# A new first-batch start, spread-out boundary scores and all squares on VectorE in a gated-attention and feed-forward kernel

## The chip, the cores and the metric

The kernel runs on one core of a Trainium2 chip. The metric is the device time of one execution in microseconds (us). Times are medians over several executions of the same build. One execution of each kernel is recorded by the hardware profiler; its span is the length of that one execution.

Names used below: PE is TensorE, DVE VectorE, ACT ScalarE, POOL GpSimd, SP the sync engine, which does nothing here but issue DMA transfers. A `q` after an engine's name (SPq, ACTq) means an instruction of its sequencer, such as the issue of a DMA.

## The reference, cut to what matters

```python
# u, v: (8, 3008, 256); z: (8, 3008, 64); w_in: (256, 2048); w_out: (2048, 256); all float32
scores = (1.0 / S) * np.matmul(z, z.transpose(0, 2, 1))
attn = np.maximum(scores, 0.0) ** 2
x = (u * np.matmul(attn, v)).reshape(B * S, D)
h = x @ w_in
g = h * (1.0 / (1.0 + np.exp(-1.702 * h)))
return (g @ w_out)
```

The scores are symmetric. The kernel computes one triangle of tiles and gets the other by DMA transposes of the squared tiles.

## The kernel before

For each of the 8 batches there are six "chunks" of 512 rows. `attend(b, i)` multiplies squared scores with V for chunk i; the scores of chunk i+1 are computed between its matmuls. Then the feed-forward of the batch runs: `up_group` (x @ w_in, sigmoid on ACT, product on DVE) and `down` (g @ w_out). The scores of the next batch's first chunk stand among the last `down` steps. PSUM is split into three double tiles (`ps2`, shared by scores and `up_group`) and two single tiles (`ps1`, for attention and `down`).

```python
def load_z(b):                                  # cast-load by POOL, then one DMA transpose
    for c in range(2):
        pool.dma_start(zst[:, :NJ - 1, c, :], zd)
        ...
    sp.dma_start_transpose(ZT[b], zst...)

def load_v(b):                                  # loads by SP, six pieces through two buffers, cast on POOL
    ...
    sp.dma_start(vst[:, :full, :], ...)
    pool.tensor_copy(V16[b]..., vst...)

def load_u(b, i):                               # four loads by SP, then a transpose on DVE
    ...
    dve.transpose(ut..., uq...)

def scores(b, group, dve_relu=False):
    for i, jp in group:                         # PE: two 64-row matmuls per unit
        sc = ps2.tile([P, 2, CH], F32, ...)
        ...
    for ...:
        act.activation(rl, sc, AF.Relu, scale=csc)      # or DVE for every third, if dve_relu
        sq[0] += 1
        (pool if sq[0] % 4 == 0 else dve).tensor_tensor(a, rl, rl, ALU.mult)
        if cj > i:                              # the mirrored tile
            sp.dma_start_transpose(t..., a...)

# program
load_z(0); load_u(0, 0); load_v(0)
for g in split(pieces(0), FIRST):               # FIRST = [3, 3, 3, 3]
    scores(0, g, True)
for k in range(P // QW):                        # weights, cast-loads by POOL
    pool.dma_start(W1[k * QW:(k + 1) * QW], w1v[k])
pool.dma_start(W2, ...)
for b in range(B):
    for i in range(NCH):                        # attention, chunk by chunk
        if i + 1 < NCH: load_u(b, i + 1)
        ...
    if b + 1 < B:
        load_z(b + 1); load_v(b + 1); load_u(b + 1, 0)
    for q in range(HEAD, nup):
        up_group(b, q)
        if q >= LAGY: down(b, *downs.pop(0))
    nxt = split(pieces(0), FIRST) if b + 1 < B else []
    n = 0
    while downs or nxt:                         # the boundary: three units, three downs, ...
        if nxt and n % 3 == 0: scores(b + 1, nxt.pop(0), True)
        if downs: down(b, *downs.pop(0))
        n += 1
```

## Time and profile before

The time before was 1306.86 us (1302.85 to 1308.07, 4 runs).

These lines are from the profile page of the kernel before: busy time by engine, the busy tenths of PE and its clock in 40 slices of the span, the chain of work that ended last, and the two groups of squares. In a group line the figures after the bar are busy time and the mean ns of one instruction, then the idle time just before them.

```profile
span 1306.3 us, 19043 instructions
PE 1249.3 (96%) x7520; PEld 680.3 (52%) x7520; DVE 844.5 (65%) x820; ACT 728.8 (56%) x786; POOL 266.9 (20%) x237
PE   2799999999999999999989999999999999999998
PEclk9799999999999999999999999999999999999999
...
PE 92%; DVE 2%; DMA 1%; POOL 1%; issue 1%; ACT 1%; ACTq 1%; SPq 0%; POOLq 0%
...
L140 POOL TENSOR_TENSOR a<-rl 128x1024 f16<-128x1024 f16 x84 | 166.2, 1979 | 717.1 <-ACT rl L136 700.2
L140 DVE TENSOR_TENSOR a<-rl 128x1024 f16<-128x1024 f16 x252 | 230.9, 939 | 98.1 <-ACT rl L136 95.1
```

PE is the bound: 96% busy and 92% of the chain. The row of digits shows PE short of work in the first two slices (65 us); shorter losses do not show there. The waits of PE, in total, say what for:

```profile
engine line waited for: us in total, times, longest us
PE sc L126 <- DMA ZT<-zst: 19.6, 1, 19.6
PE sc L126 <- ACT rl L136: 19.5, 18, 4.3
PE o L174 <- POOL V_96 L97: 5.3, 3, 2.6
PE sc L126 <- DVE gt L231: 4.8, 7, 1.0
```

To say where PE time is lost I price every useful matmul at its undisturbed distance to the next (216 ns for 512 columns and 109 ns for 256 in the trace; for N columns I take N/2.4 + 2.5 ns, which fits both), count the paired 64-row score matmuls once per pair, and count dummies and PE transposes as nothing. That gives 1202.5 us in both kernels. "Lost" below is always a stretch of the trace minus this price of the matmuls that start in it. An attention phase without any visible gap still loses 2.76 us in this account.

| lost by PE, us | before |
|---|---|
| 0 to 60 us | 45.5 |
| 60 to 120 us (rest of the first batch's attention) | 2.0 |
| 120 to 1190 us (seven boundaries and steady work) | 50.8 |
| rest | 5.5 |
| total | 103.8 |

### The profile page before, as it was taken

What the parts mean: (1) busy time and instruction counts of PE and PEld (TensorE: products, weight loads), DVE (VectorE), ACT (ScalarE), POOL (GpSimd) and SP (SyncE); (2) the same over time, 40 slices, a digit from 0 to 9 for tenths busy, and PEclk for the clock granted to TensorE, in tenths of its full rate; (3) what the DMA queues carried; (4) which work ended last, traced back from release to release, by engine and by line L of the source; (5) the groups of instructions that cost most, each with busy time, mean ns of one, the idle gap of its engine ahead of it and who ended that gap; (6) DMA issues with size and microseconds to landing.
All of it is one profiled execution on the core that took longest, in us unless ns stands there. A gap on an engine that the chain in (4) does not pass through costs nothing.

```text
span 1306.3 us, 19043 instructions
## 1 busy us (share of the span) xinstructions
PE 1249.3 (96%) x7520; PEld 680.3 (52%) x7520; DVE 844.5 (65%) x820; ACT 728.8 (56%) x786; POOL 266.9 (20%) x237
## 2 busy tenths in 40 slices
PE   2799999999999999999989999999999999999998
PEld 0244673456634566346653467444664456734566
DVE  3556777477764778647675576856776566774674
ACT  2344666356653666636665366644666446663564
POOL 4522104130131302322023220322103211041000
PEclk9799999999999999999999999999999999999999
DMA  9989518792287813878157941689408742187011
GB/s 168 201 151 173 152 49 153 136 171 84 58 168 144 146 64 88 153 149 154 40 114 147 145 133 49 127 146 138 133 33 163 142 104 83 49 154 132 1 49 49
DMA packets 483114, 153.33 MB, mean 117 GB/s; under 512 B 432080, under 2 KB 482768, under 8 KB 483024
## 3 DMA queue, kind: packets, MB, share of 16 engines
q1 hardware_dynamic: 405760, 119.07, 45.4%
q0 software_dynamic: 52304, 8.39, 8.7%
q10 hardware_dynamic: 24960, 24.65, 5.8%
q8 instruction: 59, 0.97, 0.3%
q14 instruction: 31, 0.25, 0.1%
HBM read 66.58 MB, written 24.64 MB: 70 GB/s over the span
## 4 chain that ended last, share of the span: by engine, by line
PE 92%; DVE 2%; DMA 1%; POOL 1%; issue 1%; ACT 1%; ACTq 1%; SPq 0%; POOLq 0%
PE o L174 36%; PE hg L222 25%; PE yp L245 25%; PE sc L126 6%; PE o L186 1%; DVE rl L134 1%; DVE gt L231 1%; POOL a L140 1%; DMA W_58<-in_moe_w_in_dram 1%; ACTq L260 1%; DMA zst<-in_z_dram 1%; ACT sg L230 0%; POOL V_96 L97 0%; DVE a L140 0%; DMA vst<-in_v_dram 0%
## 5 line engine op out<-in xcount | busy, mean ns | idle before, releaser
L231 DVE TENSOR_TENSOR gt<-hg,sg 128x1024 f16<-128x1024 f32 (+1 forms) x384 | 460.4, 1200 | 182.4 <-ACT sg L230 181.0
L230 ACT ACTIVATE sg<-hg 128x1024 f16<-128x1024 f32 (+1 forms) x384 | 386.0, 1005 | 274.6 <-PE hg L222 271.5
L136 ACT ACTIVATE rl<-sc 128x1024 f16<-128x1024 f32 x304 | 291.4, 1024 | 282.7 <-PE sc L126 256.0
L245 PE MATMUL yp<-W_59,gt 128*128 128x256 f16 x3008 | 383.0, 273 | 0.0
L222 PE MATMUL hg<-xt,W_58 128*128 128x512 f16 (+1 forms) x1408 | 354.5, 374 | 0.0
L245 PEld LDWEIGHTS <-gt 128*128 128x128 f16 x3008 | 292.5, 98 | 104.3 <-issue 7.5
L140 POOL TENSOR_TENSOR a<-rl 128x1024 f16<-128x1024 f16 x84 | 166.2, 1979 | 717.1 <-ACT rl L136 700.2
L140 DVE TENSOR_TENSOR a<-rl 128x1024 f16<-128x1024 f16 x252 | 230.9, 939 | 98.1 <-ACT rl L136 95.1
L222 PEld LDWEIGHTS <-W_58 128*128 128x128 f16 x1536 | 150.3, 98 | 108.7
L126 PE MATMUL sc<-ZT 64*128 64x512 f16 x672 | 104.7, 394 | 47.1 <-DMA ZT<-zst 19.6
L196 DVE TENSOR_TENSOR xt<-o,ut 128x512 f16<-128x512 f32 x80 | 55.1, 688 | 108.8 <-PE o L174 75.1
L114 DVE STREAM_TRANSPOSE ut<-uq 128x1024 f32<-128x1024 f32 (+1 forms) x48 | 58.6, 1220 | 54.1 <-DMA uq<-in_u_dram 53.2
L126 PEld LDWEIGHTS <-ZT 64*128 64x128 f16 x672 | 24.7, 95 | 115.7 <-issue 88.6
L251 ACT ACTIVATE y<-yp 128x512 f32<-128x512 f32 x96 | 56.2, 585 | 15.4 <-PE yp L245 11.5
L174 PEld LDWEIGHTS <-V_96 128*128 128x128 f16 x276 | 26.3, 100 | 43.9 <-issue 10.1
L174 PE MATMUL o<-a,V_96 128*128 128x512 f16 (+1 forms) x156 | 41.3, 411 | 5.3 <-POOL V_96 L97 5.3
L174 PEld LDWEIGHTS <-V_2475 128*128 128x128 f16 x276 | 26.3, 99 | 35.4 <-issue 7.6
L174 PEld LDWEIGHTS <-V_8743 128*128 128x128 f16 x276 | 26.1, 99 | 35.1 <-issue 7.1
L174 PEld LDWEIGHTS <-V_5609 128*128 128x128 f16 x276 | 25.9, 98 | 34.3 <-issue 5.3
L174 PEld LDWEIGHTS <-V_10321 128*128 128x128 f16 x276 | 25.9, 98 | 33.9 <-issue 5.3
L174 PEld LDWEIGHTS <-V_919 128*128 128x128 f16 x276 | 25.9, 98 | 33.9 <-issue 5.3
L174 PEld LDWEIGHTS <-V_7187 128*128 128x128 f16 x276 | 25.9, 98 | 33.9 <-issue 5.3
(55 smaller groups left out, 719.3 us busy)
## 6 DMA issues: line engine op xcount, KB each, us to landing
uq<-in_u_dram SPq DMA_DIRECT2D x160, 128.0 KB, 3.1
vst<-in_v_dram SPq DMA_DIRECT2D x40, 512.0 KB, 4.8
out_dram<-y ACTq DMA_DIRECT2D x40, 512.0 KB, 3.0
zst<-in_z_dram POOLq DMA_DIRECT2D x16, 368.0 KB, 6.7
tt<-a SPq DMA_TRANSPOSE x320, 3.2
uq<-in_u_dram SPq DMA_DIRECT2D x32, 112.0 KB, 2.5
vst<-in_v_dram SPq DMA_DIRECT2D x8, 384.0 KB, 3.6
out_dram<-y ACTq DMA_DIRECT2D x8, 384.0 KB, 4.0
```

What stands on the lines that cost most here:

```text
L114: dve.transpose(ut[:, :, :n // QW, :].rearrange("p k q t -> p q k t"), uq[:, :n // QW])
L126: pe.matmul(sc[:, r, :], zt[h, 2 * jp + r, :], zt[h, i * CB:(i + 1) * CB, :], start=True, stop=True,)
L134: dve.tensor_scalar(rl, sc, 0.0, csc, ALU.max, ALU.mult)
L136: act.activation(rl, sc, AF.Relu, scale=csc)
L140: (pool if sq[0] % 4 == 0 else dve).tensor_tensor(a, rl, rl, ALU.mult)
L174: pe.matmul(acc[c][:, :n], V16[b][:, j, c, :], weights(b, i, j), start=(c == 0 and j == 0), stop=(c == 1 and j == NJ - 2),)
L196: dve.tensor_tensor(x[:, c, :n], acc[c][:, :n], ut[:, :n], ALU.mult)
L222: pe.matmul(hg[:, e, :n], W1[:, c, ff * P:(ff + 1) * P], XT[b, i][:, c, :n], start=(c == 0), stop=(c == NCC - 1),)
L230: act.activation(sg[:, :, :n], hg[:, :, :n], AF.Sigmoid, scale=1.702 / FSC)
L231: dve.tensor_tensor(g, hg[:, :, :n], sg[:, :, :n], ALU.mult)
L245: pe.matmul(yp[:, s % 2, :], GT[b, k, ff // CB][:, ff % CB, s * P:(s + 1) * P], W2[:, ff, :], start=(ff == 0), stop=(ff == NFF - 1),)
L251: act.activation(Y[b, k][:, s0:s + 1, :], yp[:, :s % 2 + 1, :], AF.Copy, scale=1.0 / FSC)
```

## The change

It has three parts. First, the head: the first z comes in six plain loads on SP, is cast on DVE, transposed by PE and copied back by ACT, so that the scores need neither the slow cast-load nor the DMA transpose; twelve dummy matmuls warm the PE clock before; V of the first batch is issued by ACT through three buffers; the weights move behind the second chunk in program order. Second, the boundary: the next batch's first score units go into the feed-forward, in pairs between `up_group` steps (LEAD) and in two triples between `down` steps (TAIL). Third, POOL squares nothing more.

```diff
+    def warm_up(n):
+        ...
+        for k in range(n):
+            pe.matmul(w, nil[:, :P], nil, start=(k == 0), stop=(k == n - 1))
+    def first_z(g):
+        ...
+        sp.dma_start(zf[:, :full, :], z[0, n0 * P:(n0 + full) * P]...)
+        for c in range(2):
+            dve.tensor_copy(z2[:, :, c, :], zf)
+    def first_zt(g, z2):
+        zp = ps1.tile([P, CB, P], F16, name="zp", tag="ps1")
+        for k in range(CB):
+            pe.transpose(zp[:, k, :], z2[:, k, :, :], ident)
+        act.activation(ZT[0][:, g * CB:(g + 1) * CB, :], zp, AF.Copy, scale=1.0)
...
-    def load_v(b):
+    def load_v(b, eng):
-            vst = pu.tile([P, VB, D], F32, name="vst", tag="vst")
+            vst = pu.tile([P, VB, D], F32, name="vst", tag="vst", bufs=3)
-            sp.dma_start(vst[:, :full, :], ...)
+            eng.dma_start(vst[:, :full, :], ...)
...
-            sq[0] += 1
-            (pool if sq[0] % 4 == 0 else dve).tensor_tensor(a, rl, rl, ALU.mult)
+            dve.tensor_tensor(a, rl, rl, ALU.mult)
...
+    LEAD = {30: 2, 36: 2, 42: 2}
+    TAIL = {2: 3, 5: 3}
...                                  # attend(0, 0) interleaves both halves; new SCHED0 for batch 0
-    load_z(0)
+    warm_up(12)
+    fill(0)
+    z2 = [first_z(g) for g in range(NCH)]
+    load_v(0, act)
     load_u(0, 0)
-    load_v(0)
-    for g in split(pieces(0), FIRST):
-        scores(0, g, True)
-    ... weights ...
+    first_zt(0, z2[0]); take(0, 2); first_zt(1, z2[1]); take(0, 2)
+    for g in range(2, NCH):
+        first_zt(g, z2[g])
...
+            if b == 0 and i == 1:
+                ... weights ...
...
         for q in range(HEAD, nup):
+            if more:
+                take(b + 1, LEAD.get(q, 0))
             up_group(b, q)
...
+        for n in range(len(downs)):
+            if more:
+                take(b + 1, TAIL.get(n, 0), dve_relu=True)
+            down(b, *downs[n])
```

More of the change, by code (lines that the diff above doesn't have):

```diff
@@ L68 @@
     ctx.enter_context(tc.manual_schedule(engines={mybir.EngineType.PE}))
+    ident = const.tile([P, P], F16, name="ident")
+    make_identity(nc, ident)
     ZT, V16, UT, XT, unit, TT = {}, {}, {}, {}, {}, {}
+    def warm_up(n):
+        nil = const.tile([P, CH], F16, name="nil")
+        dve.memset(nil, 0.0)
+        w = ps1.tile([P, CH], F32, name="w", tag="ps1")
+        for k in range(n):
+            pe.matmul(w, nil[:, :P], nil, start=(k == 0), stop=(k == n - 1))
+    def first_z(g):
+        if g == 0:
+            ZT[0] = pz.tile([P, NJ, P], F16, name="ZT", tag="ZT")
+            ZT["st"] = pz.tile([P, NJ, 2, DQK], F16, name="zst", tag="zst")
+        if g % CB == 0:
+            ZT["f"] = pw.tile([P, CB, CB, DQK], F32, name="zf", tag="y")
+        n0 = g * CB
+        zf = ZT["f"][:, g % CB]
+        full = min(CB, NJ - 1 - n0)
+        sp.dma_start(zf[:, :full, :], z[0, n0 * P:(n0 + full) * P].rearrange("(n p) d -> p n d", p=P))
+        if full < CB:
+            for h in range(2):
+                sp.dma_start(zf[h * SREM:(h + 1) * SREM, full, :], z[0, S0:S])
+        z2 = ZT["st"][:, n0:n0 + CB]
+        for c in range(2):
+            dve.tensor_copy(z2[:, :, c, :], zf)
+        return z2
+    def first_zt(g, z2):
[3 more added lines that the diff above has]
+        act.activation(ZT[0][:, g * CB:(g + 1) * CB, :], zp, AF.Copy, scale=1.0)
     def load_z(b):
@@ L83 @@
     VB = 4
-    def load_v(b):
+    def load_v(b, eng):
         V16[b] = pz.tile([P, NJ, NCC, P], F16, name="V16", tag="V16")
         for n0 in range(0, NJ, VB):
-            vst = pu.tile([P, VB, D], F32, name="vst", tag="vst")
+            vst = pu.tile([P, VB, D], F32, name="vst", tag="vst", bufs=3)
             full = min(VB, NJ - 1 - n0)
-            sp.dma_start(vst[:, :full, :], v[b, n0 * P:(n0 + full) * P].rearrange("(n p) c -> p n c", p=P))
+            eng.dma_start(vst[:, :full, :], v[b, n0 * P:(n0 + full) * P].rearrange("(n p) c -> p n c", p=P))
             if full < VB:
                 for h in range(2):
-                    sp.dma_start(vst[h * SREM:(h + 1) * SREM, full, :], v[b, S0:S])
+                    eng.dma_start(vst[h * SREM:(h + 1) * SREM, full, :], v[b, S0:S])
             for k in range(NCC):
@@ L114, in load_u @@
         dve.transpose(ut[:, :, :n // QW, :].rearrange("p k q t -> p q k t"), uq[:, :n // QW])
-    sq = [0]
     def scores(b, group, dve_relu=False):
@@ L164, in weights, with attend, open_ @@
         return t[:, g, :, :].rearrange("p k c -> p (k c)")[:, :LAST]
-    def attend(b, i):
+    def attend(b, i, both=False):
         n = width(i)
         acc = {}
-        def mm(c, j):
-            if j == 0 and c not in acc:
-                acc[c] = ps1.tile([P, CH], F32, name="o", tag="ps1")
-            pe.matmul(
-                acc[c][:, :n], V16[b][:, j, c, :], weights(b, i, j),
-                start=(c == 0 and j == 0), stop=(c == 1 and j == NJ - 2),
-            )
-            if c == 1 and j == NJ - 2:
+        def open_(c):
+            if c not in acc:
+                acc[c] = ps1.tile([P, CH], F32, name="o", tag="ps1")
+                return True
+            return False
+        def mm(c, j):
+            new = open_(c)
+            last = c == 1 and j == NJ - 2 and not both
+            pe.matmul(acc[c][:, :n], V16[b][:, j, c, :], weights(b, i, j), start=new, stop=last)
+            if last:
                 gate(c)
         def half():
-            acc[1] = ps1.tile([P, CH], F32, name="o", tag="ps1")
             a = unit[b, i, NU - 1][:, 1, :n]
@@ L185, in half @@
                 h = slice(c * SREM, (c + 1) * SREM)
-                pe.matmul(
-                    acc[c][:, :n], V16[b][h, NJ - 1, c, :], a[h],
-                    start=(c == 1), stop=(c == 0),
-                )
-            gate(0)
+                new = open_(c)
+                pe.matmul(acc[c][:, :n], V16[b][h, NJ - 1, c, :], a[h], start=new, stop=not new)
+            for c in range(2 if both else 1):
+                gate(c)
         def gate(c):
@@ L203, in attend @@
             XT[b + 1, i] = pa.tile([P, NCC, CH], F16, name="xo", tag="xo")
-        first = [lambda j=j: mm(0, j) for j in range(NJ - 1)]
-        second = [lambda j=j: mm(1, j) for j in range(NJ - 1)]
-        return first, half, second
+        js = range(NJ - 1)
+        if both:
+            return [lambda j=j, c=c: mm(c, j) for j in js for c in range(2)] + [half]
+        return [lambda j=j: mm(0, j) for j in js] + [half] + [lambda j=j: mm(1, j) for j in js]
     GT, Y = {}, {}
@@ L277, in split, with take, fill @@
         return out_
-    FIRST = [3, 3, 3, 3]
+    LEAD = {30: 2, 36: 2, 42: 2}
+    TAIL = {2: 3, 5: 3}
     SCHED = {
-        0: [(4, 3), (14, 3), (23, 2), (34, 2)],
-        1: [(6, 3), (23, 3), (34, 2)],
-        2: [(8, 3), (23, 3)],
-        3: [(8, 2), (23, 2)],
-        4: [(23, 2)],
-        5: [],
-    }
-    load_z(0)
-    load_u(0, 0)
-    load_v(0)
-    for g in split(pieces(0), FIRST):
-        scores(0, g, True)
-    w1v = moe_w_in.rearrange("(q k c) f -> q c k f", k=NCC, c=QW)
-    for k in range(P // QW):
-        pool.dma_start(W1[k * QW:(k + 1) * QW], w1v[k])
-    pool.dma_start(W2, moe_w_out.rearrange("(fo p) c -> p fo c", p=P))
+        0: {8: 3, 15: 2, 23: 3, 34: 2},
+        1: {6: 3, 23: 3, 34: 2},
+        2: {8: 3, 23: 3},
+        3: {8: 2, 23: 2},
+        4: {23: 2},
+        5: {},
+    }
+    SCHED0 = {
+        0: {0: 2, 8: 2, 16: 2, 24: 2, 32: 3, 40: 3},
+        1: {0: 2, 8: 2, 15: 3, 23: 3, 34: 2},
+        2: SCHED[2], 3: SCHED[3], 4: SCHED[4], 5: {},
+    }
+    queue = []
+    def take(b, n, **kw):
+        if n:
+            group = [queue.pop(0) for _ in range(n)]
+            scores(b, group, **kw)
+    def fill(b):
+        assert not queue
+        queue.extend(u_ for i in range(NCH) for u_ in pieces(i))
+    warm_up(12)
+    fill(0)
+    z2 = [first_z(g) for g in range(NCH)]
+    load_v(0, act)
+    load_u(0, 0)
+    first_zt(0, z2[0])
+    take(0, 2)
+    first_zt(1, z2[1])
+    take(0, 2)
+    for g in range(2, NCH):
+        first_zt(g, z2[g])
     for b in range(B):
         nup = NCH * NFG
+        sched = SCHED if b else SCHED0
         for i in range(NCH):
-            first, half, second = attend(b, i)
-            steps = first + second
-            groups = dict(zip([p for p, _ in SCHED[i]], split(pieces(i + 1) if i + 1 < NCH else [], [n for _, n in SCHED[i]])))
             if i + 1 < NCH:
@@ L308 @@
             h = 0
-            for n, step in enumerate(steps):
-                if n in groups:
-                    scores(b, groups[n])
-                if n == NJ - 1:
-                    half()
+            for n, step in enumerate(attend(b, i, both=(b == 0 and i == 0))):
+                take(b, sched[i].get(n, 0))
                 if i == NCH - 1 and n % 5 == 2 and h < HEAD:
@@ L317 @@
                 step()
-        if b + 1 < B:
+            if b == 0 and i == 1:
+                w1v = moe_w_in.rearrange("(q k c) f -> q c k f", k=NCC, c=QW)
+                for k in range(P // QW):
+                    pool.dma_start(W1[k * QW:(k + 1) * QW], w1v[k])
+                pool.dma_start(W2, moe_w_out.rearrange("(fo p) c -> p fo c", p=P))
+        more = b + 1 < B
+        if more:
             load_z(b + 1)
-            load_v(b + 1)
+            load_v(b + 1, sp)
             load_u(b + 1, 0)
+            fill(b + 1)
         downs = down_list(b)
         for q in range(HEAD, nup):
+            if more:
+                take(b + 1, LEAD.get(q, 0))
             up_group(b, q)
@@ L326 @@
                 down(b, *downs.pop(0))
-        nxt = split(pieces(0), FIRST) if b + 1 < B else []
-        n = 0
-        while downs or nxt:
-            if nxt and n % 3 == 0:
-                scores(b + 1, nxt.pop(0), True)
-            if downs:
-                down(b, *downs.pop(0))
-            n += 1
+        for n in range(len(downs)):
+            if more:
+                take(b + 1, TAIL.get(n, 0), dve_relu=True)
+            down(b, *downs[n])
 _INS = ['u', 'v', 'z', 'moe_w_in', 'moe_w_out']
```

## The prediction

> **What bounds the kernel now.** TensorE: the page gives PE 96% busy, and the chain of waits is 92% PE. In steady state 512-column matmuls start 216 ns apart, 256-column ones 109 ns. All 7520 matmuls at that rate, with the paired 64-row score matmuls counted once per pair, make about 1202 us. So about 104 of the 1306 us are lost on PE. By PE start times in the timeline:
>
> - Head, 0 to 60 us: about 46 us lost. The first score matmul waits until 19.6 us for ZT (cast-load of z, then a DMA transpose issued at 11.8). PE then waits for relus, squares and V casts (gaps of 4.8, 2.8, 2.8, 2.0 us), and matmuls start 427 ns apart until about 54 us; the granted clock reads 0.64 and 0.68 in 40-50 and 50-60. That agrees with the Trainium skill, "TensorE: Matmul & The Clock Gate", Part 1.
> - Seven batch boundaries: about 3.3 us of gaps on even ones (0.7, 0.6, 0.5, 0.7, 0.7 near 190-204), about 5 on odd ones (1.2, then 2.6 at 360, where ACT waited for a square on POOL, followed on two of three by 3.4 us at half clock). Sum about 29 us.
> - The rest is small and untouched.
>
> **Head after.** No software-queue load nor DMA transpose before the first scores. z piece 0 (128 KB; uq of that size lands in 3.1 us) lands at 4-6 us. Cast on DVE, four PE transposes, ACT copy of about 0.6 us: first scores at 7-9 us. But attend(0,0) opens both ps1 banks, so it waits until ACT has copied out all six transposed pieces, beside four relus: 6 x 0.6 + 4 x 1.02 = 7.7 us. ACT also issues V in order and may block on vst buffers. I expect attend to start at 15-17 us. The dummies (12 x 0.43 = 5 us) warm the clock, but the gap until attend probably cools it: 2 us lost. attend(0,0) with its 14 score units is 13 us of PE; V (3 MB at about 200 GB/s, done near 20 us) should not hold it. Head loss about 18 us: gain about 28.
>
> **Boundaries after.** Relus and squares of 12 units are spread out. Each LEAD pair takes the two free ps2 tiles, so the next up_group waits for the previous gt, as the third score unit does now (1.1 us for 512-wide blocks, 0.65 for 384): about 3 us per boundary. TAIL groups find three free tiles, and the gaps inside attend vanish, with the cold windows. Gain about 0.5 on even, 2 on odd boundaries: 8 us in all.
>
> **Squares.** POOL takes 1979 ns, DVE 0.69 us undisturbed. DVE's mean is 939 because squares overlapping a POOL one stretch to 1.57-2.4 us; the Trainium skill, "GPSIMD Engine Reference", 1. Specifications, says the two share SBUF interfaces, and the trace agrees. DVE gets 84 x 0.69 = 58 us more but loses about 60 us of stretching: busy unchanged, off the critical path. Its worth is already in the odd boundaries.
>
> **Sum.** 1306.6 - 28 - 8 = about 1271 us, 8 in 10: 1259 to 1286. Faster by over 2%: 0.83; within: 0.16; slower: 0.01.
>
> **What would show it.** First attend matmul at 15-17 us; no half clock after 20 us; PE loss before 60 us near 18. Gaps of about 1.1 us before up_group after each LEAD take, waiting for DVE gt; none near 2.6 us in attend. DVE squares near 0.7 us.
>
> **What would make it wrong.** ACT blocked by V issues (later attend); V bandwidth shared with u, z and the hoisted next z; LEAD takes disturbing the up/sigmoid/gt pipeline for several groups.

## The result, and the profile after

The changed kernel took 1305.93 us (1303.95 to 1306.19, 4 runs), against 1306.86 before. The ratio is 0.9995, 95% interval 0.9971 to 1.0018: the same time.

The profile page of the kernel after, the same lines:

```profile
span 1304.2 us, 19129 instructions
PE 1249.4 (96%) x7556; PEld 682.2 (52%) x7556; DVE 823.0 (63%) x899; ACT 748.7 (57%) x810; POOL 96.4 (7%) x149
PE   5789999999999999999999999999999999999998
PEclk7899999999999999999999999999999999999999
...
PE 88%; DMA 4%; DVE 3%; ACT 3%; issue 1%; SPq 1%; ACTq 0%; DVEq 0%
...
L173 DVE TENSOR_TENSOR a<-rl 128x1024 f16<-128x1024 f16 x336 | 227.0, 690 | 120.3 <-ACT rl L170 119.8
```

And the waits of PE after, the five largest:

```profile
PE hg L259 <- DVE gt L268: 13.4, 14, 1.0
PE sc L160 <- ACT ZT L106: 9.9, 2, 9.2
PE o L215 <- DVE a L173: 7.6, 2, 6.4
PE hg L259 <- ACT rl L170: 6.3, 7, 0.9
PE o L215 <- DVE xt L232: 4.5, 1, 4.5
```

The old waits are gone and new ones of about the same sum stand in their place: all waits of PE together are 52.4 us before and 49.1 after. The third digit of the PE row shows where the gain at the start went: the first two slices rose from 2 and 7 to 5 and 7, and the third fell from 9 to 8. DMA rose from 1% to 4% of the chain.

| lost by PE, us | before | after |
|---|---|---|
| 0 to 60 us | 45.5 | 34.5 |
| 60 to 120 us | 2.0 | 10.6 |
| 120 to 1190 us | 50.8 | 50.6 |
| rest | 5.5 | 5.9 |
| total | 103.8 | 101.7 |

The boundaries split further. Attention of batches 1 to 7 lost 35.8 us before and 22.7 after. The feed-forwards of batches 0 to 6 lost 15.6 before and 28.3 after. So two expected gains, each real at its own place, were given back next door.

The head of the kernel after, first on PE, then on ACT's own instructions (columns: start, duration, instruction, count, idle time before it and what ended it):

```profile
7.58 0.61 PE L160 MATMUL sc<-ZT 64*128 64x512 f16 x4 [0.69 <-ACT ZT L106]
8.11 0.40 PE L105 MATMUL zp<-ident,zst 128*128 128x128 f16 x4
17.74 1.03 PE L160 MATMUL sc<-ZT 64*128 64x512 f16 x4 [9.23 <-ACT ZT L106]
...
22.84 1.48 PE L215 MATMUL o<-a,V_124 128*128 128x512 f16 x4
...
43.68 2.72 PE L215 MATMUL o<-a,V_124 128*128 128x512 f16 x6 [6.44 <-DVE a L173]
```

```profile
6.92 0.60 ACT L106 ACTIVATE ZT<-zp 128x512 f16<-128x512 f16 x1 [3.19 <-PE zp L105]
11.59 2.31 ACTq L128 DMA_DIRECT2D vst<-in_v_dram  x3
13.94 1.28 ACTq L131 DMA_DIRECT2D vst<-in_v_dram  x2
15.26 1.94 ACT L170 ACTIVATE rl<-sc 128x1024 f16<-128x1024 f32 x2 [7.74 <-issue]
```

The first scores come at 7.58 us instead of 19.57. Then PE waits 9.23 us for ACT, and ACT did nothing for 7.74 us: its instructions run in order, and the issues of the last V pieces stood in front of the first relu. About 4 us of this is ACT waiting to issue, the rest the issues and shorter waits between them. By the trace, what ended these waits was not a V buffer (the casts of the first piece were done at 6.66 us) but the landing of earlier loads: of the third V piece at 11.48 us, then of two pieces of z at 12.37 and 13.44. The first attention matmul comes at 22.84 us (32.47 before).

### The profile page after: what moved, and what is told of

It is laid out like the page before. It is cut to its first block, busy times and chain, and to the rows that moved or that the text cites. A ratio compares the mean times of both kernels' runs of the same rounds, so it can differ in the third digit from the quotient of the medians.

```text
span 1304.2 us, 19129 instructions
## 1 busy us (share of the span) xinstructions
PE 1249.4 (96%) x7556; PEld 682.2 (52%) x7556; DVE 823.0 (63%) x899; ACT 748.7 (57%) x810; POOL 96.4 (7%) x149
## 4 chain that ended last, share of the span: by engine, by line
PE 88%; DMA 4%; DVE 3%; ACT 3%; issue 1%; SPq 1%; ACTq 0%; DVEq 0%
PE o L215 34%; PE hg L259 25%; PE yp L282 24%; PE sc L160 5%; DVE gt L268 1%; ACT sg L267 1%; DMA uq<-in_u_dram 1%; ACT rl L170 1%; DVE a L173 1%; DMA vst<-in_v_dram 1%; PE o L224 1%; DMA tt<-a 1%; DMA zf<-in_z_dram 1%; SPq L187 0%; SPq L147 0%
## 5 line engine op out<-in xcount | busy, mean ns | idle before, releaser
L170 ACT ACTIVATE rl<-sc 128x1024 f16<-128x1024 f32 x322 | 308.4, 1024 | 250.8 <-PE sc L160 232.4
L173 DVE TENSOR_TENSOR a<-rl 128x1024 f16<-128x1024 f16 x336 | 227.0, 690 | 120.3 <-ACT rl L170 119.8
L259 PEld LDWEIGHTS <-W_58 128*128 128x128 f16 x1536 | 150.1, 98 | 136.5 <-issue 28.2
L160 PE MATMUL sc<-ZT 64*128 64x512 f16 x672 | 99.0, 385 | 12.5 <-ACT ZT L106 9.9
L113 POOL DMA_DIRECT2D zst<-in_z_dram x14 | 21.3, 1524 | 732.3 <-DMA ZT<-zst 732.3
L288 ACT ACTIVATE y<-yp 128x512 f32<-128x512 f32 x96 | 56.1, 585 | 27.9 <-PE yp L282 24.5
```

The lines of the kernel that those rows point to most:

```text
L160: pe.matmul(sc[:, r, :], zt[h, 2 * jp + r, :], zt[h, i * CB:(i + 1) * CB, :], start=True, stop=True,)
L173: dve.tensor_tensor(a, rl, rl, ALU.mult)
L259: pe.matmul(hg[:, e, :n], W1[:, c, ff * P:(ff + 1) * P], XT[b, i][:, c, :n], start=(c == 0), stop=(c == NCC - 1),)
L288: act.activation(Y[b, k][:, s0:s + 1, :], yp[:, :s % 2 + 1, :], AF.Copy, scale=1.0 / FSC)
```

## The experiments

All runs computed the right result. "Lost before attention" is PE time lost before the first attention matmul, "batch 0" is what attention of batch 0 lost from there.

### Group 1: the parts of the change, one at a time

**Squares on DVE alone**, on the kernel before:

```diff
-            sq[0] += 1
-            (pool if sq[0] % 4 == 0 else dve).tensor_tensor(a, rl, rl, ALU.mult)
+            dve.tensor_tensor(a, rl, rl, ALU.mult)
```

> The kernel before with one edit: all squares on VectorE. Theory A (the squares are the useful half of the boundary work): the waits of ACT for a POOL square at the odd batch boundaries (2.6 to 3.0 us at 360, 676, 991) and the half-clock windows behind them vanish, even boundaries lose a little less; total 1296 to 1301 us. Rival B (VectorE takes over as the thing waited for): 1304 to 1309 us, gaps of the same size waiting for a DVE square. Head loss in 0-60 us should stay within 3 us of 45.5 in both.

Measured: 1306.87 us (1306.57 to 1309.06), ratio 0.999 (0.9964 to 1.0016). The 336 squares on DVE took 694 ns each. Attention of batches 1 to 7 lost 32.7 instead of 35.8 us and the feed-forwards 13.8 instead of 15.6, but batch 0's attention lost 22.6 instead of 17.8. So the squares are worth about 5 us at the boundaries in this trace, and batch 0's attention took most of it back (a single trace of it is good to about 4 us only, see below).

Theory A failed where it named the waits. The gaps of PE at the three odd boundaries stayed: 2.7, 2.1 and 2.2 us here, 2.3, 2.7 and 2.7 before. So a square on POOL was not what they waited for. ACT and PE at the first of them, in this run:

```profile
362.33 2.44 ACTq L259 DMA_DIRECT2D out_dram<-y  x2
364.88 3.77 ACT L136 ACTIVATE rl<-sc 128x1024 f16<-128x1024 f32 x4 [2.12 <-DVE rl L134]
365.96 1.02 PE L126 MATMUL sc<-ZT 64*128 64x512 f16 x4 [2.69 <-ACT rl L136]
```

After every second batch ACT issues two more output DMAs, for the last rows that two batches share. At all three odd boundaries ACT's next relu starts 0.1 us after these issues end; they take 1.9 to 2.4 us here, 2.1 to 2.4 in the kernel before and 1.8 to 2.4 in e2. The profile names other releasers for these relus (DVE's relu here, nothing or a square of DVE elsewhere). That the issues hold ACT is read from the order and the times; no run moved them.

**The change with the old boundary** (new head, squares on DVE):

```diff
-    LEAD = {30: 2, 36: 2, 42: 2}
-    TAIL = {2: 3, 5: 3}
+    LEAD = {}
+    TAIL = {0: 3, 3: 3, 6: 3, 9: 3}
-        0: {8: 3, 15: 2, 23: 3, 34: 2},
+        0: {4: 3, 14: 3, 23: 2, 34: 2},
```

> The changed kernel with the old batch boundary (four groups of three score units among the last down projections, old first schedule), new head and VectorE squares kept. If the spread score units (LEAD pairs) are what gave back the boundary gain: feed-forward loss per batch falls from 4.05 to about 2 us, and attention loss of batches 1 to 7 stays at 2.8 to 4 us; total 1294 to 1300 us. If the boundary gain of the changed kernel came from spreading and not from the squares: attention loss of batches 1 to 7 goes back to 4 to 7 us, total 1304 to 1310 us.

Measured: 1305.58 us (1304.17 to 1306.07), ratio 0.9975 (0.995 to 1.0). Attention of batches 1 to 7 and feed-forwards together lost 32.5 + 13.8 = 46.3 us; with the new boundary it is 22.7 + 28.3 = 51.0. The new boundary is 4.7 us worse than the old one, once the squares are on DVE in both. The total does not show it, because batch 0's attention lost 28.2 us in this trace instead of 23.8.

**No dummies:**

```diff
-    warm_up(12)
```

> The changed kernel without its 12 dummy matmuls. Theory: [...]the dummies buy nothing: total within 1.5 us of the changed kernel (1304 to 1307), first attention matmul still at 22 to 24 us. Rival: they keep the transposes and first scores quick: 2 to 4 us slower.

Measured: 1307.66 us (1307.14 to 1309.74), ratio 0.9996 (0.997 to 1.0021). Batch 0's attention lost 2.0 us more, the rest hardly moved. That is within the scatter of such traces, and the ratio too does not tell the dummies from nothing. Half clock is on record from 10.1 us after the change.

**Score units one at a time between the up groups:**

```diff
-    LEAD = {30: 2, 36: 2, 42: 2}
+    LEAD = {27: 1, 30: 1, 33: 1, 36: 1, 39: 1, 42: 1}
```

> The changed kernel with the six early score units of the next batch taken one at a time (before up groups 27, 30, 33, 36, 39, 42) in place of three pairs. Theory: a pair takes both free PSUM tiles, so each pair costs 1.2 us (three per boundary); a single takes one, and the next up group finds the other: stalls under 0.3 us, feed-forward loss per batch from 4.05 to 1.0 to 1.5 us, total 1283 to 1288 us. Rival (ACT is simply short of time there, 1.02 us more for each unit): the stalls split into six of about 0.6 us, total 1303 to 1307 us.

Measured: 1291.14 us (1288.96 to 1293.92), ratio 0.9873 (0.9841 to 0.9906). The feed-forwards lost 11.9 instead of 28.3 us: 1.70 instead of 4.05 at each boundary. These are PE's instructions around a LEAD take, first after the change, then in this run:

```profile
158.34 0.60 PE L160 MATMUL sc<-ZT 64*128 64x512 f16 x4
159.91 1.02 PE L259 MATMUL hg<-xt,W_58 128*128 128x512 f16 x4 [0.96 <-DVE gt L268]
```

```profile
153.62 0.39 PE L160 MATMUL sc<-ZT 64*128 64x512 f16 x2
153.97 1.02 PE L259 MATMUL hg<-xt,W 128*128 128x512 f16 x4
```

A pair leaves the next up group to wait 0.96 us for the product that frees its PSUM tile; a single unit leaves no wait. In the waits of PE after the change the two lines of `hg` sum to 19.7 us in 21 waits, three per boundary; in this run neither of them is among the waits listed. This settles the cost of the pairs. The sizes missed a little: 1.70 us a boundary where 1.0 to 1.5 was expected, and a time 3 us above the range.

### Group 2: the start

**V pieces 3 to 5 issued by POOL instead of ACT:**

```diff
+            eng = pool if issuer is act and n0 >= 3 * VB else issuer
```

> The changed kernel with the last three of the six first V loads issued by POOL in place of ACT; ACT then issues only the three that need no wait. Theory (ACT stood still from 7.5 to 15.3 us in its queue behind those V issues): ACT copies piece 1 of ZT by about 9 to 11 us, the 9.4 us gap of PE before the second pair of scores falls under 4 us, first attention matmul at 15 to 18 us in place of 22.8. Total: 5 to 7 us less if nothing later gives it back (1298 to 1301); if the later waits for u set the pace, the gain is lost by 46 us and the total stays 1304 to 1307. Rival (z itself comes late because V shares the DMA): the gap stays above 7 us.

Measured: 1297.46 us (1294.78 to 1298.82), ratio 0.9923 (0.9906 to 0.9941). ACT's first relu came at 7.87 us instead of 15.26, and the first attention matmul at 15.59, inside the 15 to 17 us that the prediction had. Lost before attention: 14.3 instead of 21.6 us. Batch 0 lost 23.8 us, as after the change. So the blocked ACT is confirmed and worth 7 us. But PE now waited 10.5 us for one transpose:

```profile
57.13 1.87 PE L217 MATMUL o<-tt,V 128*128 128x512 f16 x4 [10.53 <-DMA tt<-a]
```

**Weights and next z held back**, by small POOL copies that need an early attention result:

```diff
             if b == 0 and i == 1:
+                pool.tensor_copy(W1[:, 0, :1], XT[0, 1][:, 0, :1])
+                pool.tensor_copy(W2[:, 0, :1], XT[0, 1][:, 0, :1])
...
+            if b == 0 and i == 2:
+                held = const.tile([P, 1], F16, name="held")
+                pool.tensor_tensor(held, ZT["st"][:, 0, 0, :1], XT[0, 2][:, 0, :1], ALU.mult)
```

> The changed kernel with both weight loads held back until the gate of chunk 1 and the next batch's z until the gate of chunk 2 (tiny POOL copies that read those gates' results). Theory C (these loads crowd u, V and the transposes off the DMA rings between 27 and 50 us): u of chunk 1 lands by 32 us in place of 41.8, the 6.7 us gap of PE at 36.9 vanishes; head loss in 0-60 falls from 34.5 to about 27 and the loss in 60-120 from 10.6 to about 4; total 1290 to 1297 us. Rival D (issue order on SP alone makes u late): the gap stays at 5 us or more, total 1303 to 1307.

Measured: 1302.33 us (1300.45 to 1304.47), ratio 0.9964 (0.9947 to 0.9981). The time fell between the ranges of the two theories: 0 to 60 us lost 24.0 us instead of 34.5, but 60 to 120 us lost 18.6 instead of 10.6. The trace is the plainest of all. POOL issued the weights at 47.6 to 51.1 us and the next z at 60.0 to 65.2. The view of the transposed tiles on SP, first for 26 to 47 us, then for 47 to 70 us (duration of one issue in ns, least, median and longest):

```profile
L181 SPq DMA_TRANSPOSE tt<-a x10: 1231/1286/2320, 25.8 to 46.7; - x10
L187 SPq DMA_TRANSPOSE tt<-a x4: 1217/1241/1259, 33.7 to 37.6; - x4
```

```profile
L181 SPq DMA_TRANSPOSE tt<-a x4: 1231/2282/3962, 46.7 to 68.7; - x4
L187 SPq DMA_TRANSPOSE tt<-a x4: 1860/2290/8502, 49.5 to 62.5; - x4
who waited for it (us, times):
  PE o L215: 13.1, 1
```

With no load of the software queue (the loads that POOL issues) in flight, the median issue of a transpose takes 1.24 to 1.29 us. Beside the weights and the next z the median is 2.3 us and the longest 8.5, and PE stood for 13.1 us. Holding the loads to 47 us moved the collision, it did not remove it.

**The transposes of u late in DVE's order** (because in the trace after the change DVE stood 9.95 us before a u transpose while squares waited behind it):

```diff
-        dve.transpose(ut..., uq...)
+        def tr(): dve.transpose(ut..., uq...)
+        if b == 0 and i < 5: late[i] = ut, tr
...
+                if b == 0 and n == (43 if i == 0 else 17):
+                    late_ut(i)
```

> The changed kernel with the u transposes of the first batch placed later in VectorE's order (a tiny copy that reads a late square goes ahead of each). Theory: squares stood behind a u transpose that waited for its load (6.4 and 9.9 us idle on DVE), so the 6.7 us gap of PE at 36.9 and the 4.7 us gap at 88 vanish or shrink to under 2 us: total 1294 to 1299 us. Rival: the late load is needed soon after by the gate anyway, and the same time is lost at the first matmul of the next chunk, waiting for DVE xt: total 1302 to 1306.

Measured: 1312.96 us (1312.21 to 1313.29), ratio 1.0044 (1.0029 to 1.0059). Batch 0 lost 30.3 us. The 6.4 us wait for a square went, and waits for gates (6.3), for the next z's transpose (6.2) and for one transposed tile (5.0) came. A miss.

**All three together** (V by POOL, loads held, u late; the edits of e5, e6 and e7):

> All three head edits together (V by POOL, weights and next z held back, u transposes late). If the three causes are the whole of the missing head gain: first attention matmul at 15 to 18 us, head loss in 0-60 about 20 us, 60-120 about 3 us, total 1278 to 1287 us. If something else bounds the head (V arriving at the DMA rate, half clock), the loss in 0-60 stays above 28 us.

Measured: 1311.18 us (1309.69 to 1311.75), ratio 1.0032 (1.0016 to 1.0049). Lost before attention 13.9 us, batch 0 35.7. PE waited 11.5 us for one transposed tile and 9.1 for the next z's transpose. A miss again: attention starts 7.6 us earlier, and 12 us more is lost behind it.

### Group 3: next z, and issue by other engines

**Next z only after the last chunk but one has its gate**, with the change as it is (e9), with V by POOL as in e5 (e10), and with the single units of e4 too (e11). Added in all three:

```diff
+            if b == 0 and i == 4:
+                held = const.tile([P, 1], F16, name="held")
+                pool.tensor_tensor(held, ZT["st"][:, 0, 0, :1], XT[0, 4][:, 0, :1], ALU.mult)
```

> The changed kernel with one edit: the next batch's z is not loaded until the gate of chunk 4 of the first batch (about 90 us), by a tiny POOL multiply that keeps the old z buffer busy until then; weights and V untouched. Theory F (the first batch's attention is paced by DMA engine time: u, V, weights, the square transposes and this load together take 129 us of the 16 engines in 122 us, and the transposes that the next chunk needs stand behind them): 12 us of DMA work leave, transposes between 33 and 52 us issue faster, attention loss of batch 0 falls from 23.8 to 12 to 17 us, total 1293 to 1300. Rival (late u from issue order, VectorE blocked): attention loss of batch 0 stays above 21 us, total 1303 to 1307.

> V by POOL and the late z together. Theory F: the 10.7 us gap at 46 us of the V-by-POOL run (waiting for a square transpose[...]) vanishes: attention loss of batch 0 from 23.8 to 10 to 14 us, start of attention stays at 15 to 16 us, total 1284 to 1290. Rival (the weight loads, not z, hold the transposes): the gap stays at 6 us or more, total above 1292.

> V by POOL, late z and single early score units: the version meant to beat both kernels. If the three repairs add up: 1306 - 8 (V) - 10 (z) - 16 (singles) = 1272, range 1266 to 1278; about 2.6% faster than the kernel before. If the repairs share one cost: 1280 to 1287.

Measured: e9 1301.6 us (1299.03 to 1302.92), ratio 0.9953 (0.994 to 0.9967); e10 1298.21 (1297.24 to 1299.71), 0.9931 (0.9917 to 0.9944); e11 1282.88 (1278.39 to 1286.86, 5 runs), 0.9805 (0.9789 to 0.9821). Batch 0 lost 20.9, 20.5 and 24.5 us. In e9 that is 2.9 us less than after the change, within the scatter of such traces. e10 was no faster than e5 (0.9931 against 0.9923), and its longest wait for a transposed tile was 4.9 us instead of 10.5; its time is above 1292, as the rival had it. e11 fell in its second range, 1280 to 1287: the repairs did not add up. In e10 and e11 the first feed-forward lost 1.9 and 4.1 us more than in the same kernels without the late z, because z was then late for the boundary. So moving the next z alone does not repair the start.

**The same on the kernel before:**

> The kernel before with only the late z. Theory F says that DMA time paced the head before the change too (141 us of DMA work in the first 124 us): attention loss of batch 0 falls from 17.8 by 4 to 8 us, total 1299 to 1303. If the load only hurt the changed kernel's order of work: within 2 us of 1307.

Measured: 1311.7 us (1309.69 to 1311.86), ratio 1.0029 (1.0016 to 1.0043). Batch 0 lost 17.1 us instead of 17.8, though its transposes ended at 101.0 us instead of 105.6; the first feed-forward lost 8.2 us more; the time is outside both expectations. The timeline of the kernel before shows no idle time of PE between 60 and 125 us, so earlier transposes had nothing to give there.

**u of the first batch issued by POOL instead of SP**, with the change (e13), on the kernel before (e14), and with V by POOL and single units (e15). This takes the loads of u off the list of SP, which was busy for 95% of the stretch from its first to its last transpose:

```diff
-            sp.dma_start(uq[...]...)
+            (pool if b == 0 and i else sp).dma_start(uq[...]...)
```

> The changed kernel with the u loads of chunks 1 to 5 of the first batch issued by POOL in place of SP (which also puts the next z behind them in POOL's queue; the late-z run is the control for that). Theory G (the first batch's attention is paced by SP's one in-order list: 40 square transposes of about 1.6 us and 20 u loads of 0.6 us, 94% busy from 26 to 103 us): SP is rid of 12 us, the last transpose ends by 88 to 94 us, attention loss of batch 0 falls from 23.8 to 12 to 16 us, total 1294 to 1299. Rival F (DMA engine time, which does not change when another queue issues the same bytes): attention loss stays above 20 us, total 1301 to 1307.

> The same edit on the kernel before. Theory G says its first batch was paced by the same list (first transpose at 25.1 us, last ends at 105.6, 94% busy): attention loss of batch 0 falls from 17.8 to about 10 us, total 1297 to 1302. Rival: within 2 us of 1307.

> u and V by POOL and single early score units, natural place of the next z. If theory G holds and V by POOL lets the transposes start at 16 us: start loss 14, attention loss of batch 0 10 to 14, feed-forward loss 12 in all: total 1268 to 1276 us. If SP's list is not the pacer: 1279 to 1285, as the run with late z and singles.

And, for comparison with e15, **V by POOL and single units alone**, u left on SP (the edits of e4 and e5):

> V by POOL and singles alone, as the control of the run before: the sum of their separate gains (8 and 15 us) gives 1280 to 1285 us under every theory.

Measured: e13 1308.49 us (1306.93 to 1310.35), ratio 1.0005 (0.9986 to 1.0023); e14 1306.9 (1304.51 to 1308.47), 0.9986 (0.9966 to 1.0005); e15 1290.68 (1287.19 to 1292.61), 0.9865 (0.9844 to 0.9886); e16 1283.96 (1281.55 to 1287.67), 0.9819 (0.9793 to 0.9845). In e13 SP had some 12 us less to issue, yet its transposes ended at 109.4 us instead of 103.0: one took 2.01 us on average instead of 1.58. In e15 it was 2.01 against 1.83 in e16, and the kernel was slower. On the kernel before (e14) the mean went from 1.45 to 1.54 us, though the last transpose ended earlier, at 99.3 us instead of 105.6, and the time stayed the same. None of the totals that theory G gave came. A theory in which SP's list of issues is simply too long does not hold: the list was made shorter and the transposes took longer. The Trainium skill, "DMA: Bandwidth & Descriptors", "Issuing engines are not separate DMA queues", says that issuing from several engines saves only the sequencer's issue time; these runs show no more than that, and after the change even that saving was lost.

### Group 4: the weights and the next z away from the first transposes

By now the open question was whether the transposes are stretched by loads in flight beside them, or whether the first 120 us are held by a total of DMA work that has to be done anyway. Two runs were made for it. **e17** is e16 with the weights and the next z both held until the gate of chunk 4. The first `up_group` steps, which need the weights, were moved later too. The late pieces of V still went by the software queue, until about 23 us:

```diff
-                if i == NCH - 1 and n % 5 == 2 and h < HEAD:
+                if i == NCH - 1 and n % 5 == 2 and h < HEAD and (b or n > 25):
...
-            if b == 0 and i == 1:
+            if b == 0 and i == 4:
+                held = const.tile([P, 1], F16, name="held")
+                pool.tensor_tensor(held, ZT["st"][:, 0, 0, :1], XT[0, 4][:, 0, :1], ALU.mult)
+                pool.tensor_copy(W1[:, 0, :1], XT[0, 4][:, 0, :1])
+                pool.tensor_copy(W2[:, 0, :1], XT[0, 4][:, 0, :1])
                 ... weights ...
```

> V issued by GpSimd, weights and next z both held until the last chunk of the first batch, up groups of the first batch correspondingly late, lead units singly. Theory (software-queue loads stretch the transposes): transposes of the first batch go at 1.3 to 1.6 us each on the sync queue from about 25 us on, attention of the first batch loses at most 12 us, 1265 to 1277 us in all. Rival (total DMA work or the sync engine's list holds it): attention of the first batch still loses 20 us or more, 1279 us or more in all. The late weights may cost some us at the first feed-forward; that is read apart from the attention.

**e18** is the change with the weights issued at the very start, as the kernel before had them:

```diff
+    for k in range(P // QW):                 # before fill(0)
+        pool.dma_start(W1[k * QW:(k + 1) * QW], w1v[k])
+    pool.dma_start(W2, ...)
...
-            if b == 0 and i == 1:
-                ... weights ...
```

> The changed kernel with the weights issued at the very start, as the kernel before had it. Theory: attention starts later (25 to 30 us instead of 22.8, since z and V share the queues with the weights), but the transposes are stretched less, so the first batch's attention loses 15 to 18 us after its start-up is counted apart; within 5 us of 1306 in all. Rival (place of the weights does not matter to the transposes): attention starts later and nothing is won back, 1310 us or more.

Measured: e17 1280.02 us (1278.57 to 1282.05, 4 runs), ratio 0.9803 (0.9785 to 0.9822). e18 1303.44 us (1303.1 to 1304.19), ratio 0.9983 (0.9964 to 1.0002).

The view of the transposed tiles on SP for 20 to 60 us, of e16 and then of e17:

```profile
L183 SPq DMA_TRANSPOSE tt<-a x11: 1242/2876/6352, 17.8 to 58.9; - x11
...
  PE o L217: 11.4, 1
...
DMA to landing us min/median/max: 3.2/8.0/14.6
```

```profile
L183 SPq DMA_TRANSPOSE tt<-a x16: 1254/1288/2194, 21.4 to 57.4; - x16
L189 SPq DMA_TRANSPOSE tt<-a x9: 1216/1238/1589, 31.4 to 58.8; - x9
...
DMA to landing us min/median/max: 2.4/3.3/6.0
```

The issues are back at 1.24 to 1.29 us (medians), the tiles land in 3.3 us instead of 8.0, PE waits for none of them, and the last transpose ends at 82.6 us instead of 101.2. PE lost 18.8 us up to 60 us (31.9 in e16). From 90 to 120 us it lost 10.0 (2.8 in e16), because the weights now came late:

```profile
PE hg L261 <- DMA W<-in_moe_w_in_dram: 4.1, 1, 4.1
PE o L217 <- DVE xt L234: 3.4, 2, 2.8
```

In all, batch 0 lost 16.3 us, between the 12 of one expectation and the 20 of the other, and 1280.02 us is 3 us above the range of my theory and 1 us inside that of the rival. By its total this run would not decide, and my figure for the total missed. By the transposes it does: they were stretched by the loads beside them. POOL now issued these at 83.8 to 92.6 us, after the last transpose; none was taken away. Whether sharing as such or the time of the DMA engines being used up in the first 60 us does the stretching, this run does not separate.

e18 says the same more weakly. Attention started at 23.82 us, sooner than the 25 to 30 us of the theory; the 1310 us of the rival did not come. The mean transpose took 1.44 us instead of 1.58, the last ended at 101.5 us instead of 103.0, and batch 0 lost 20.9 us instead of 23.8, within the scatter; the expectation was 15 to 18. Its next z and part of its V were still in flight beside the first transposes, one of which took 4.7 us.

### What the runs say together

| run | mean transpose of batch 0, us | last one ends | lost before attention | batch 0 |
|---|---|---|---|---|
| before | 1.45 | 105.6 | 29.9 | 17.8 |
| after | 1.58 | 103.0 | 21.6 | 23.8 |
| e5 V by POOL | 1.75 | 97.4 | 14.3 | 23.8 |
| e9 z late | 1.52 | 100.3 | 21.5 | 20.9 |
| e13 u by POOL | 2.01 | 109.4 | 21.6 | 29.2 |
| e16 V by POOL, singles | 1.83 | 101.2 | 14.7 | 28.2 |
| e17 e16, weights and z late | 1.38 | 82.6 | 13.5 | 16.3 |
| e18 weights first | 1.44 | 101.5 | 22.5 | 20.9 |

The mean counts the transposes that SP issued after the first attention matmul of batch 0, 38 to 40 of them. In the second and third batch of each of these kernels, where the weights and V are no longer loaded beside them, it is 1.30 to 1.36 us. Over all 20 kernels the loss of batch 0's attention and the sum of these transposes have a correlation of 0.77; without e7 and e8, which also reordered DVE, 0.89. That is a correlation; what shows the cause is e6 within one trace and e17 against e16.

## Why the prediction was wrong, point by point

**What bounds the kernel** was right: PE, and 46 us lost before 60 us (45.5 by the later account).

**Squares** were right in DVE's time and wrong in what they were worth. The prediction had 0.69 us on DVE undisturbed, and the group line after says 690 ns, against a mean of 939 before; DVE's busy time was predicted as unchanged and went from 844.5 to 823.0 us. The Trainium skill, "GPSIMD Engine Reference", 1. Specifications, says that GpSimd shares its SBUF interfaces with VectorE; the trace agrees: before the change the 86 squares on DVE that overlap one on POOL took 1427 ns on average and the other 166 took 686, and removing POOL's squares shortened DVE's own. What failed is "Its worth is already in the odd boundaries": the waits there were not for POOL (e1).

**First scores** were right: 7 to 9 us predicted, 7.58 measured.

**Attention start** was wrong: "I expect attend to start at 15-17 us", and it came at 22.84. The prediction named the risk, "ACT also issues V in order and may block on vst buffers", and gave it no time. (The waits ended with the landing of earlier loads, not with a free buffer.) It cost 7 us: with the blocked V pieces issued elsewhere (e5) attention started at 15.59. The step that failed is the cost of a blocked issue on an engine that also has work on the critical path.

**The head's gain of 28** was the step that failed most. It took for granted that the head ends when attention starts and that PE then has its operands. "PE loss before 60 us near 18" came out as 34.5, and the stretch from 60 to 120 us, which no term of the sum had, went from 2.0 to 10.6. The gain up to 120 us was 47.6 - 45.1 = 2.4 us (unrounded sums). What the first batch's attention needs next comes through SP's list of issues: the mirrored tiles by their DMA transposes, and the loads of u between them. That list did not get earlier with PE. The first transpose was issued at 26.4 us (25.1 before), the issue of the eighth ended at 52.4 (52.9 before), the last ended at 103.0 (105.6 before). From 20 to 60 us the issues were stretched before the change (first line) and after it (second line); the third line is DVE after the change:

```profile
L148 SPq DMA_TRANSPOSE tt<-a x9: 1262/2054/5829, 25.1 to 59.4; - x9
L181 SPq DMA_TRANSPOSE tt<-a x10: 1231/2272/6008, 26.4 to 59.7; - x10
41.81 1.25 DVE L150 STREAM_TRANSPOSE ut<-uq 128x1024 f32<-128x1024 f32 x1 [9.95 <-DMA uq<-in_u_dram]
```

In the trace after the change PE itself waited only 1.8 us for transposed tiles. Its waits of 6.4 and 4.5 us came through DVE, which stood 9.95 and 8.65 us for loads of u: the last one for chunk 1 was issued at 30.9 us and took 10.9 us to land (those issued after 57 us took 2.2 to 3.9; one of chunk 1 in the kernel before took 11.8), those behind the second wait were issued only at 85.0 to 87.1 us, behind transposes.

What was in flight beside the first transposes changed, but there were such loads before as well. After the change POOL issued the weights at 1.3, 12.7 and 25.8 us and the next z from 27.5 to 32.7; the last packet of V had ended at 23.5. Before, the first weight matrix was issued by 9.3 us, the second at 24.2 and the next z from 42.6, and V was landing until 47.8. The prediction did list "V bandwidth shared with u, z and the hoisted next z" as a risk; but it is the transposes and the loads of u that suffered, and V was not what PE waited for. The Trainium skill, "DMA: Bandwidth & Descriptors", Queues, rings and completion order, says that each DMA engine goes round-robin between the queue rows at packet granularity. That fits, if what the trace calls packets are the page's: after the change a 4096-byte packet of the software queue took 385 ns on average in the trace and a 256-byte one of SP's queue 22 ns, so a transpose that takes turns with such packets gets slow. That the turns are the mechanism is argued, not shown; that the loads beside them stretch the transposes is shown by e6 and e17. With both causes out of the way, the blocked ACT and the loads beside the transposes (e17), PE lost 18.8 us before 60 us, about what the prediction had.

**The clock** was wrong in "no half clock after 20 us". After the change the clock records show half clock from 10.1 to 23.8, 40.8 to 47.7 and 92.0 to 95.5 us. Each of the three begins during one of the three long waits of PE; it followed the wait and did not cause it. The Trainium skill, "TensorE: Matmul & The Clock Gate", Part 1, gives N / 1.2 GHz per matmul for a cold array; the dummies, 427 ns apart at 512 columns, agree.

**Boundaries** were wrong: a gain of 8 us was predicted, 51.4 - 51.1 = 0.3 came (unrounded sums). The prediction's sum was that about 29 us of gaps go and "about 3 us per boundary" for the LEAD pairs come, 21 in all. The pairs measured 1.23 + 1.23 + 1.17 = 3.6 us, 25.4 in all, so by difference about 25.7 us went: the cost was taken too small and the gaps too large. Attention lost 13.0 us less, 3.0 of it by the squares alone (e1). The whole feed-forward loss per boundary was 4.05 us instead of 2.2 before: 12.7 us given back. The old kernel paid such a wait once per boundary (0.48 or 0.96 us, 4.8 us in 7 waits), the new one pays 0.9 to 0.96 us three times. e4 shows that the pairing costs this: the same units one at a time took 16.4 us off the feed-forwards.

**What stays open.** How the stretching divides between weights, next z, V and u is not settled; in e13 the same u loads stretched the transposes more when POOL issued them, and why is not shown (these loads went as packets of 4096 bytes there, 832 of these in the trace instead of 256, and as packets of 256 bytes on SP's queue). That the two output issues of ACT make the gaps at the odd boundaries is not shown either. e5 and e16 differ only in the boundary, yet batch 0 lost 23.8 and 28.2 us in their traces, so a single trace of the first batch is good to about 4 us only. Whether a stretched issue is time spent in moving data or in waiting for room in the queue, the trace does not say.

**Versions that beat both kernels.** e17 (V pieces 3 to 5 by POOL, single LEAD units, weights and next z behind the transposes) is the best by its median, 1280.02 us, ratio 0.9803 (0.9785 to 0.9822); e11 (1282.88, 0.9805) and e16 (1283.96, 0.9819) lie within each other's intervals. All three are faster than the kernel before, but whether by 2% or more is unclear. e17 still waits 4.1 us for the weights; a release one chunk earlier would be the next thing to try and was not run.

## What to carry to other kernels

When a start is made faster, follow every producer that the next phase needs, not just the first operand of the bounding engine: here TensorE was fed 10 us earlier while the DMA transposes and the loads of u that it needs later kept their old schedule, slowed by other loads beside them. Keep DMA issues that may have to wait out of the queue of an engine whose compute is on the critical path; here that cost 7 us. When filler work shares a rotating PSUM pool with a pipeline, add it one tile at a time; the same six units cost 4.05 us per boundary with pairs and 1.70 with singles.

## What the Trainium skill lacked or had wrong

- "DMA: Bandwidth & Descriptors", DMA Transpose (X-bar): no time of an SBUF-to-SBUF transpose beside ordinary loads. Here the median issue of one (a 128x1024 fp16 tile, or half of it) takes 1.24 to 1.29 us with no software-queue load beside it, and one took 8.5 us beside such loads (e6), and the median time to landing goes from 3.3 to 8.0 us (e17 against e16).
- The same page, "Issuing engines are not separate DMA queues": it says that the issuing engine only saves issue time. Moving the loads of u from SP to GpSimd made SP's transposes slower, 1.58 to 2.01 us on average (e13 against the changed kernel, one trace of each; 1.83 to 2.01 in e15 against e16). Which queue a load uses seems to matter to what runs beside it, and the page has no number for that.
- "TensorE: Matmul & The Clock Gate", Part 4: it has about 275 ns for one PE transpose of 128x128 in a kernel. Single ones are recorded here with 219 to 314 ns, which agrees, but in a row they start 107 ns apart at half clock (from 18.7 us) and 56 to 66 ns apart at full clock (from 8.1 us); the page has no rate in a row.
- "GPSIMD Engine Reference", 1. Specifications: it names the shared SBUF interfaces but gives no size for element-wise work like this. Here DVE's squares took 939 ns on average with a quarter of them on POOL and 690 ns with none.
- No page that I read has the cost of a blocked DMA issue on an engine that also computes: here ACT computed nothing for 7.74 us.
